# Two token tiles' k and v by seven block products in a fused attention and dense kernel

## The chip, the cores and the metric

The kernel runs on one core of a Trainium2 chip. The metric is the device time of one execution in microseconds (us), taken as the median of several runs. The core's engines work side by side, each on its own queue of instructions: PE (matrix multiply, with a separate record PEld for loading the stationary operand), DVE (vector), ACT (scalar functions), POOL (the general-purpose engine) and SP, whose queue issues nearly all DMA transfers here. PE writes into PSUM, which has eight banks of 128 partitions by 2 KB; all other on-chip data lie in SBUF.

## The reference

The input x has 2048 tokens of width 512. It is normalised per token (mean and variance over the 512 columns) and goes into two branches whose results are multiplied and added to x:

- Branch A, linear attention with 32 heads of width 16: `q, k, v = xn @ wqkv`; q and k are multiplied per head by a 16x16 matrix `w_phi`; `phi = [softmax(p), softmax(-p)]` per head, 32 values; `kv = sum over tokens of phi_k^T v` and `z = sum over tokens of phi_k`; then `num = phi_q kv`, `den = phi_q z + 1e-6`, `s = (num / den) @ wo`.
- Branch B, a dense layer: `h = xn @ w1 + b1` (1792 columns), `mish(h) @ w2`, and `silu` of that is g.
- The result is `x + s * g`.

Inputs and result are float32.

## The kernel before

**Numbers in two halves.** A float32 operand of a big matmul is kept as two tiles, high and low (`split`, line 429: ACT copies the value into the rounded type, and a subtraction gives the rest). Three matmuls (low by high, high by low, high by high) then make one exact enough product. They have the form 128x128 by 128x512. A product over the whole contraction of 512 is 4 blocks times 3, so 12 matmuls.

**The parts.** There are 16 token tiles of 128 tokens. The program is a list of parts named in the string `ORDER` (line 36), each of which records instructions:

- `wk`, `wv`, `wq`, `wo`: weights loaded, folded with `w_phi` where needed (PE), and split.
- `N t`: loads x of tile t, normalises it, transposes it on PE into the PSUM tile `pt`, splits it into the tile `xT`, copies it once more whole (`xr`), and writes the whole copy and the two halves to HBM (`raw`, `scr`).
- `K t`, `V t`, `Q t`: a projection of 12 matmuls each (`proj`, line 529). K and Q are followed by `softmax` (line 538): a copy `p` of the logits out of PSUM, a maximum and a minimum per head, two subtractions (on DVE from PSUM, or on POOL from the copy), the exponential on ACT, sums and reciprocals; for K also the scaling. `Q t` first reads its tile of xn back from HBM (`xq`).
- `A p`: for two consecutive tiles, adds phi_k to the sum `zacc` and multiplies v with phi_k into the PSUM bank `kvp` by small matmuls. `z` finishes both sums.
- `D t`: denominators, scaled phi_q, transposed on DVE in blocks of 32 into the tile `ph`, which holds four token tiles and exists once.
- `Ua g`, `Ub g`: the numerators of four token tiles in two halves of 64 small matmuls (32x32 by 32x128), then their split out of PSUM.
- `O t`: multiplication with `wo`; the result goes to HBM.
- `P b`, `M b`: w1 of two column blocks loaded, its four block sums made and split (`P`), and the halves read back from HBM later (`M`).
- `L q`: for 1024 tokens, loads xn from HBM: three blocks in halves, four blocks whole; from the whole ones four block sums are made and split.
- `Fa`, `Fb`, `Fc`, `Fd` n: the first dense layer by Strassen's scheme in Winograd's form: seven block products in place of eight, each 6 matmuls; sums of products are formed by accumulating in PSUM and by an addition on DVE (`plus`). `Fa` to `Fd` of one n hold 2, 2, 1 and 2 of the seven products.
- `R`, `G`, `E`: w2, the second dense layer with mish, and the final combination and output.

**What sets the order.** A planner in the file (`Program`) walks the parts in the order of the list. PE executes its matmuls exactly in that order. For every other instruction the planner simulates the engines with a cost per operation (line 62), gives each a due time from the PE instruction that needs it, and chooses, where an operation may run on either of two engines (`either`, `copy`), the engine. It also counts the buffers: 38 of 4 KB (`slot`), 11 of 2 KB (`s2`), 8 PSUM banks, and some smaller ones. The simulation's order is what is issued; at run time every queue is worked off in that order. All instructions are issued from one line (345), so the profile groups them by tile names.

Of the kernel before, what the change touches and what calls it, by code (L numbers as in the profile page):

```python
# [17 lines left out]
P = 128  # L18
# [14 lines left out]
SLOTS, S2 = 38, 11  # L33
# [3 lines left out]
wk0 wv1 wv0 wq0 N2 N1 P3 N0 wk1 K0 N9 N3 K2 V1 K1 V3 V2 K3 N5 N4 V0 K4 wq1 K5 A0 N8 V5 K8 K9 V4 N7 A1 P2 A2 V9 K7 N6  # L37
V8 V6 P0 N11 K6 A4 L0 V7 N10 N12 Fa3 K10 Fa0 V12 A3 V10 V11 K11 Fb3 Fb0 Fc3 Fc0 N13 N14 Fd3 K12 P6 V13 N15 P5 Fd0 K14
A5 V15 V14 K15 K13 Fa6 Fb6 Fa5 M2 Fc6 Fa2 P4 Fd6 Q5 P1 Fa4 Q2 Fb2 b1 Q1 Fc2 A6 A7 Fd2 Fa1 Fb4 Fc4 Q0 z Fb5 D1 Fb1 Fc1
D0 Q13 Q3 M4 L1 Fc5 Fd1 Q7 Q4 D4 Fd5 Q9 M0 M6 Fd4 Fa9 Fb9 Fa11 Fb11 Fc9 D3 Fc11 Fd9 Fd11 Fa7 D9 Fb7 D2 M5 D5 Fa13 Fb13  # L40
Fc13 Fc7 Fd13 Fa12 M1 Fd7 Ua0 wo0 Q6 D7 Fa8 D6 Ub0 R0 Fb8 Fb12 Fc8 Fc12 Fd8 Q8 Q12 D13 R1 Q15 wo1 M3 Fa10 Fd12 Fb10
Ua1 Fc10 Q10 Ub1 Fd10 Q14 R5 D8 D10 O0 G7 D14 O7 O4 R4 O6 G8 R2 O1 G12 Q11 O5 G9 O2 R3 G0 G3 G10 G11 R6 G13 O3 D12 D11
G1 Ua2 E1 G5 G4 G2 G6 E0 D15 G14 Ub2 G16 G15 Ua3 G18 Ub3 G19 O10 G17 O12 G20 O15 O13 O11 G21 O8 O9 O14 E2 G24 G25 G23
G22 G26 E3
# [4 lines left out]
class Op:  # L49
    __slots__ = ("impl", "reads", "writes", "at", "idx", "succ", "ndep", "late", "new", "ready", "start", "eng", "sets", "slack", "open", "soon", "pos", "deps", "lock", "part", "half", "code")  # L50


class Program:
# [53 lines left out]
    def call(self, e, m, a, k):  # L107
        aps = [v for v in list(a) + list(k.values()) if isinstance(v, bass.AP)]
        w = {aps[0].tensor.name}
        r = {v.tensor.name for v in aps[1:]}  # L110
# [36 lines left out]
    def links(self):  # L147
        ops = self.ops
        wr, rd = {}, {}
        for o in ops:  # L150
            o.succ, dep = [], set()
            for n in o.reads:
                dep.update(wr.get(n, ()))
            for n in o.writes:
                dep.update(wr.get(n, ()))
                dep.update(rd.get(n, ()))
# [6 lines left out]
            for n in o.reads:  # L163
                rd.setdefault(n, []).append(o.idx)
            for n in o.writes:
                wr.setdefault(n, []).append(o.idx)
        self.uses, self.first = {}, {}
        for o in ops:
            o.new = []
            for n in o.reads | o.writes:  # L170
                if n in self.tag:
                    self.uses[n] = self.uses.get(n, 0) + 1
                    if n not in self.first:
                        self.first[n] = o
                        o.new.append(n)

    def simulate(self, at):
# [103 lines left out]
        while left:  # L281
# [8 lines left out]
            for kind, i in todo:  # L290
# [6 lines left out]
                elif kind == 1:  # L297
                    o = ops[i]
                    left -= 1
                    for n in o.reads | o.writes:  # L300
                        if n in uses:
                            uses[n] -= 1
                            if uses[n] == 0:
                                free[self.tag[n]] += 1
# [11 lines left out]
            for e in ("A", "V", "G", "Q"):  # L316
                if busy[e] > now or e == "Q" and (dma > now + BACK or lanes[-LANES:][0:1] > [now] and len(lanes) >= LANES):
                    continue
                skip = []
                while ready[e]:  # L320
# [11 lines left out]
                    if len(skip) > 60:  # L332
                        break
# [4 lines left out]
    def issue(self):  # L338
        first = True
        for o in self.order():  # L340
            for m, a, k in o.impl[o.eng][1]:
# [3 lines left out]
                getattr(e, m)(*a, **k)  # L345

# [24 lines left out]
def block_kernel(ctx: ExitStack, tc: tile.TileContext, x, wqkT, wv, phi, wo, w1, b1, w2, out):  # L371
# [9 lines left out]
    for tag, n in (("slot", SLOTS), ("s2", S2), ("sm", 13), ("rq", 5), ("st", 3 * NT), ("tq", 1)):  # L381
        pools[tag] = ctx.enter_context(tc.tile_pool(name=tag, bufs=n))
        prog.cap[tag] = n
# [55 lines left out]
    vb = [const.tile([P, D], F32, name=f"v{i}") for i in range(4)]  # L439
# [29 lines left out]

    def fold(wT, name, i):  # L470
        hi = slot([P, 2, D], f"{name}h{i}", F32R)
        lo = slot([P, 2, D], f"{name}l{i}", F32R)
        for j in range(2):
            ps = bank([P, D], f"{name}f{i}{j}")
            with one():
                for g in range(KC):
                    PE.matmul(ps[:, g * P:(g + 1) * P], wT[2 * i + j][:, g, :], phit[:, g, :], start=True, stop=True)
            split(ps, hi[:, j, :], lo[:, j, :])
# [15 lines left out]
    scr = [dram.tile([P, 2, KC, 4, P], F32, name=f"scr{g}") for g in range(NG)]  # L494
# [411 lines left out]
```

## Time and profile before

| | |
|---|---|
| median of three runs | 521.39 us (521.24 to 522.45) |
| span of the profiled execution, first to last instruction | 520.4 us |
| its own time with what lies around the span | not recorded; the median of the runs is 1.0 us above the span |
| busy share of the span: PE, DVE, ACT, POOL | 98%, 72%, 52%, 50% |
| DMA | 120.33 MB, 231 GB/s on average |
| granted PE clock | 0.998 |

How to read it. Busy time is the time in which an engine has an instruction under way; matmuls overlap, so their mean duration (some 390 ns for 128x512) is longer than their distance. Rows of groups read: line, engine, operation, output<-inputs, shapes, count | busy us, mean ns of one | idle time of the engine just before them and what ended it. In rows of stretches each engine has its busy time in us and the number of instructions (x), then the granted clock of PE, the busy share of the DMA engines, and GB/s. The chain is the work that ended last, followed backwards; its rows are start us, length us, what.

### The profile page before, as it was taken

The numbers are of one execution on the slowest core, as the hardware profiler recorded it, in microseconds if no ns is written. First come the engines' busy times: TensorE is split into PE (matmuls) and PEld (weight loads), VectorE is DVE, ScalarE is ACT, GpSimd is POOL, SyncE is SP. The second block draws the span as 40 slices with busy tenths as digits, with TensorE's granted clock in tenths as the row PEclk, the third lists the DMA queues.
The fourth block names the chain that finished last, engine by engine and source line by source line (L and its number), as shares of the span: only waits on it lengthen the run. The fifth ranks groups of instructions, "written<-read, shape, count | busy, mean of one in ns | idle before, by whom it ended". The sixth has DMA issues, their size and how long they took to land.

```text
span 520.4 us, 9655 instructions
## 1 busy us (share of the span) xinstructions
PE 510.9 (98%) x3764; PEld 420.9 (81%) x3764; DVE 376.7 (72%) x531; ACT 270.8 (52%) x386; POOL 260.4 (50%) x160
## 2 busy tenths in 40 slices
PE   8998999999999999999999999999999999999996
PEld 8787878888888878878888878888888887888885
DVE  5999998898898977989877989957457373214304
ACT  4854566464443433552234586776496773296001
POOL 2669899677778555947543868622433310000000
PEclk9999999999999999999999999999999999999999
DMA  8888799929889789789987855674466233245802
GB/s 311 297 284 236 273 305 305 340 72 339 283 270 339 267 268 357 233 309 312 309 277 254 277 180 194 231 262 162 152 226 231 102 102 105 81 164 180 282 2 81
DMA packets 84557, 120.33 MB, mean 231 GB/s; under 512 B 7073, under 2 KB 49441, under 8 KB 84513
## 3 DMA queue, kind: packets, MB, share of 16 engines
q1 hardware_dynamic: 84368, 119.70, 68.1%
q8 instruction: 29, 0.48, 0.4%
q14 instruction: 16, 0.12, 0.1%
q10 hardware_dynamic: 144, 0.03, 0.0%
HBM read 71.08 MB, written 48.63 MB: 230 GB/s over the span
## 4 chain that ended last, share of the span: by engine, by line
PE 80%; DVE 11%; ACT 3%; POOL 2%; DMA 2%; issue 2%; ACTq 0%; POOLq 0%; DVEq 0%
PE y L345 30%; PE fx L345 13%; PE pw L345 8%; PE fy L345 6%; PE q L345 6%; PE v L345 4%; PE k L345 4%; PE fz L345 3%; PE pn L345 3%; DMA fr<-raw 2%; DVE nb L345 1%; PE wake L345 1%; PE kvp L345 1%; POOL zacc L345 1%; DVE xT L345 1%
## 5 line engine op out<-in xcount | busy, mean ns | idle before, releaser
L345 ACT ACTIVATE r<-r,b1t 128x512 f32<-128x512 f32 x56 | 38.3, 718 | 8.4 <-DMA r<-hd 8.3
L345 PE MATMUL k<-wkh,xT 128*128 128x512 f32 x128 | 42.4, 395 | 0.2 <-DVE rs L345 0.2
L345 PE MATMUL q<-wqh,xq 128*128 128x512 f32 x128 | 41.5, 390 | 0.0
L345 DVE TENSOR_TENSOR u<-u,sr 128x512 f32<-128x512 f32 (+1 forms) x14 | 10.0, 714 | 42.0 <-ACT u L345 39.5
L345 ACT ACT_TABLE_LOAD x23 | 29.5, 1283 | 1.6 <-PEq L898 1.2
L345 ACT ACTIVATE u<-y 128x512 f32<-128x512 f32 (+1 forms) x17 | 9.7, 573 | 38.5 <-PE y L345 38.4
L345 PEld LDWEIGHTS k<-wkh,xT 128*128 128x128 f32 x128 | 24.0, 188 | 6.1 <-DVE xT L345 0.8
L345 PEld LDWEIGHTS q<-wqh,xq 128*128 128x128 f32 x128 | 24.0, 188 | 5.2 <-issue 0.2
L345 PE MATMUL k<-wkl,xT 128*128 128x512 f32 x64 | 25.1, 392 | 0.0
L345 PE MATMUL q<-wql,xq 128*128 128x512 f32 x64 | 24.9, 389 | 0.0
L345 PE MATMUL v<-wv0h,xT 128*128 128x512 f32 x64 | 23.2, 403 | 0.4 <-DVE xT L345 0.4
L345 PE MATMUL v<-wv1h,xT 128*128 128x512 f32 x64 | 22.4, 390 | 0.0
L345 ACT ACTIVATE so<-pw 128x512 f32<-128x512 f32 x12 | 7.1, 596 | 26.0 <-PE pw L345 24.2
L345 DVE TENSOR_REDUCE tz<-ez 128x64 f32<-128x1024 f32 x16 | 19.2, 1198 | 0.2
L345 DVE TENSOR_TENSOR ol<-pn,oh 128x256 fp32r<-128x256 f32 x32 | 12.0, 413 | 10.1 <-ACT oh L345 10.0
L345 ACT ACTIVATE oh<-pn 128x256 fp32r<-128x256 f32 x32 | 10.6, 390 | 14.6 <-PE pn L345 9.2
L345 POOL TENSOR_TENSOR rs<-rs,mhalf 128x1 f32<-128x1 f32 x16 | 9.8, 618 | 16.1 <-DVE rs L345 16.1
L345 ACT ACTIVATE v<-v 128x512 f32<-128x512 f32 x16 | 9.4, 590 | 15.3 <-PE v L345 15.3
L345 DVE COPY so<-pw 128x512 f32<-128x512 f32 x4 | 2.8, 692 | 18.5 <-PE pw L345 18.5
L345 POOL TENSOR_TENSOR w1sl<-w1s,w1sh 128x1024 fp32r<-128x1024 f32 x5 | 12.0, 2404 | 8.3 <-ACT w1sh L345 6.8
L345 ACT ACTIVATE ha<-fx 128x512 f32<-128x512 f32 x14 | 8.4, 599 | 14.9 <-PE fx L345 12.1
L345 ACT ACTIVATE hc<-fx 128x512 f32<-128x512 f32 x14 | 8.3, 595 | 14.7 <-PE fx L345 11.8
(805 smaller groups left out, 1785.4 us busy)
## 6 DMA issues: line engine op xcount, KB each, us to landing
r<-hd SPq DMA_DIRECT2D x28, 512.0 KB, 3.8
scr<-xT SPq DMA_DIRECT2D x16, 512.0 KB, 4.8
xq<-scr SPq DMA_DIRECT2D x16, 512.0 KB, 5.4
w1b<-w1d SPq DMA_DIRECT2D x14, 512.0 KB, 5.5
w1b<-w1d SPq DMA_DIRECT2D x14, 384.0 KB, 4.7
x<-x SPq DMA_DIRECT2D x16, 256.0 KB, 4.9
raw<-xr SPq DMA_DIRECT2D x16, 256.0 KB, 4.4
fr<-raw SPq DMA_DIRECT2D x8, 512.0 KB, 7.5
```

The lines of the kernel that those rows point to most:

```text
L345: getattr(e, m)(*a, **k)
```

## The change

**k and v of two tiles by seven products.** Tiles t and t+4 form a pair. With the two halves of the contraction and with k and v as the two column halves, the eight block products become the seven of the scheme that the dense layer uses already (`kv_product`, parts `Ka`, `Kb`, `Kc`, `Kd` of pair p with 2, 2, 1 and 2 products). k of each tile and v of one get one addition (`plus`) of a PSUM bank to the copy in SBUF. The weights' four block sums are made and split in new parts `ws0` to `ws3`; they lie in the buffer `tq`, which later holds `ph`.

**x sums at norm time.** The four block sums of xn for a pair of tiles are made in `sums_x` from the PSUM tiles of both, split, kept for `Kb` to `Kd`, and written to HBM (`scrT`). `L` then only loads: three blocks and four sums, each in halves, 14 transfers of 512 KB. The whole copies `raw` are gone; the layout of `scr` is turned so that a tile's halves are contiguous.

**q logits through HBM.** `Q t` multiplies with the tile's own `xT` (no reading back of xn), copies the logits and writes them to HBM. A new part `S t` reads them and does the softmax. The softmax takes its input always from the SBUF copy, so both subtractions read SBUF, whether on DVE or on POOL.

**Numerators for eight tiles.** `ph` holds eight token tiles (32 KB). `U n` makes the numerators of half of the heads for eight tiles: 64 small matmuls 32x32 by 32x256, so there are four such parts in place of eight.

**Order and planner.** The list of parts is new. The planner now tracks which part of a tile is read and written (`box`, `meet`), and looks further past waiting operations. v tiles come from a pool of four buffers; a DMA scratch area is reduced to make room.

```
-SLOTS, S2 = 38, 11
+SLOTS, S2, RQ = 38, 11, 5
...
+wv0 wk0 wv1 ws0 N0 N1 wk1 ws1 N4 wq0 N5 Ka0 Kb0 N2 ws2 wq1 Ka1 Kc0 Q2 Ka2 N8 N6 ws3 Kd0 N3 Q5 N7 Q8 Kb1 Kc1 Q4 Ka3 N12
+Kb2 Kc2 Q0 Ka4 N9 P2 Kd2 A0 b1 Kd1 Q3 N13 N10 Q1 N11 Q6 P0 Kb3 Q13 N14 Kb4 A1 Kc3 Q10 Kc4 N15 Kd3 P1 Q7 Ka6 A2 P3 Q9
+Ka7 S4 Ka5 A3 Q14 Q11 Kd4 Kb5 Q15 Kc5 Kb6 Q12 Kd5 Kb7 Kc6 Kc7 S6 L0 A4 Fa3 P6 Kd7 Fb3 Kd6 A5 Fc3 S7 Fd3 Fa0 Fa1 Fb1 P4
+Fc1 A6 Fd1 S0 Fa4 A7 z P5 S1 D0 Fa5 M2 Fa2 Fb4 Fa6 D1 Fb0 Fc0 S2 S3 Fb6 Fd0 Fb2 Fc4 Fc6 Fd4 S5 Fb5 D2 D3 M1 L1 Fc5 Fd6
+M6 Fa9 D4 Fa8 Fc2 Fb9 Fd5 D5 Fb8 wo0 wo1 D6 M0 Fd2 Fc8 Fc9 Fd8 D7 Fd9 Fa13 U1 Fb13 Fc13 M4 U0 Fd13 S8 Fa7 O6 O1 Fb7 R2
+R0 O0 Fc7 O5 O3 O4 O7 O2 Fa11 S10 Fb11 M3 Fc11 S14 Fd7 Fa10 G7 Fd11 R3 D8 M5 R1 Fb10 Fc10 S9 D9 Fa12 R5 Fb12 Fc12 Fd10
+Fd12 R4 G0 G1 G2 G3 S11 D10 D11 S12 G8 G4 D12 S15 G9 G10 G5 R6 G6 E0 G11 S13 G12 G14 D13 G15 D14 G16 D15 G13 G17 U2 E1
+G18 U3 G19 O12 O8 O10 O14 G20 G21 G22 O15 O9 G23 O11 O13 G24 G25 E2 G26 E3
...
-    scr = [dram.tile([P, 2, KC, 4, P], F32, name=f"scr{g}") for g in range(NG)]
-    raw = [dram.tile([P, KC, 4, P], F32, name=f"raw{g}") for g in range(NG)]
+    scr = [dram.tile([P, 4, 2, KC, P], F32, name=f"scr{g}") for g in range(NG)]
+    scrT = [dram.tile([P, 4, 2, 4, 2, P], F32, name=f"scrT{q}") for q in range(2)]
+    qd = [dram.tile([P, D], F32, name=f"qd{t}") for t in range(NT)]
...
         split(pt, w[:, 0], w[:, 1])
-        xT[t] = w
+        xT[t], pts[t] = w, pt
+        g, i = divmod(t, 4)
+        Q.dma_start(scr[g][:, i], f32(w))
+        if g % 2:
+            sums_x(t - 4)
+
+    def sums_x(t):
+        p1, p2 = pts.pop(t), pts.pop(t + 4)
         xr = s2(f"xr{t}")
-        copy(xr, pt.rearrange("p k n -> p (k n)"))
-        Q.dma_start(raw[t // 4][:, :, t % 4, :], xr.rearrange("p (k n) -> p k n", k=KC))
-        Q.dma_start(scr[t // 4][:, :, :, t % 4, :], f32(w))
+        copy(xr, p2.rearrange("p k n -> p (k n)"))
+        xr = xr.rearrange("p (k n) -> p k n", k=KC)
+        ts = slot([P, 4, 2, P], f"ts{t}")
+        V.tensor_tensor(ts[:, 0], xr[:, 0:2], p1[:, 0:2], op=ALU.subtract)
+        with one():
+            V.tensor_tensor(ts[:, 1], p2[:, 2:4], ts[:, 0], op=ALU.subtract)
+            G.tensor_tensor(ts[:, 1], xr[:, 2:4], ts[:, 0], op=ALU.subtract)
+        with one():
+            V.tensor_tensor(ts[:, 2], p2[:, 2:4], xr[:, 0:2], op=ALU.subtract)
+            G.tensor_tensor(ts[:, 2], xr[:, 2:4], xr[:, 0:2], op=ALU.subtract)
+        V.tensor_tensor(ts[:, 3], p1[:, 2:4], ts[:, 1], op=ALU.subtract)
+        th, tl = (slot([P, 4, 2, P], f"t{n}{t}", F32R) for n in "hl")
+        split(ts, th, tl, either)
+        tT[t] = th, tl
+        g, i = divmod(t, 4)
+        for j, u in enumerate(tT[t]):
+            Q.dma_start(scrT[g // 2][:, i, j], f32(u))
...
+    def kv_product(ps, t, a, n, first):
+        (ah, al), (xh, xl) = w["kv"][a], combo(t, n)
+        with one():
+            for k in range(2):
+                for i, (u, v) in enumerate(((xl, ah), (xh, al), (xh, ah))):
+                    PE.matmul(ps, u[:, k], v[:, k], start=first and k == 0 and i == 0, stop=k == 1 and i == 2, skip_group_check=True)
...
-        with one():
-            V.tensor_tensor(e[:, :, 0, :], ps3, hi, op=ALU.subtract)
-            G.tensor_tensor(e[:, :, 0, :], p3, hi, op=ALU.subtract)
...
+        either(e[:, :, 0, :], p3, hi, op=ALU.subtract)
+        either(e[:, :, 1, :], lo, p3, op=ALU.subtract)
...
+    def kv_a(p):
+        t = tile_of(p)
+        x, z = bank([P, D], f"kx{p}"), bank([P, D], f"kz{p}")
+        kv_product(x, t, 0, 0, True)
+        kp[t] = held(x, f"kp{t}")
+        kv_product(z, t, 1, 1, True)
+        plus(kp[t], z)
+        k_soft(t)
+        kx[p] = [x]
...
     def q_proj(t):
-        xT[t] = slot([P, 2, KC, P], f"xq{t}", F32R)
-        Q.dma_start(f32(xT[t]), scr[t // 4][:, :, :, t % 4, :])
+        p = s2(f"qs{t}")
+        copy(p, proj(t, w["q"], "q"))
+        Q.dma_start(qd[t], p)
+
+    def q_soft(t):
+        p = s2(f"qp{t}")
+        Q.dma_start(p, qd[t])
...
+    def num(n):
+        q, i = divmod(n, 2)
+        ph = phT[q]
+        pn = [bank([P, 2, 2 * P], f"pn{n}_{b}") for b in range(4)]
...
+        fx[q] = [combo(f"b{n}", lambda u: scr[2 * q + g][:, :, u, 2 * k:2 * k + 2]) for n, g, k in ((0, 0, 0), (1, 0, 1), (2, 1, 1))]
+        fx[q] += [combo(f"t{n}", lambda u: scrT[q][:, :, u, n]) for n in range(4)]
...
-                    PE.matmul(ps, u[:, a % 3 if a < 3 else a - 3, c], v[:, k, :], start=first and k == 0 and i == 0,
+                    PE.matmul(ps, u[:, a % 3 if a < 3 else a - 3, c], v[:, :, k, :], start=first and k == 0 and i == 0,
...
+    def weights_s(i):
+        x, y, op = ((vr[0], vr[1], ALU.add), (sr[0], kr[0], ALU.subtract), (kr[0], vr[0], ALU.subtract), (kr[1], sr[1], ALU.subtract))[i]
+        sr[i] = slot([P, 2, D], f"ws{i}")
+        either(sr[i], x, y, op=op)
+        if "ws" not in w:
+            w["ws"] = alloc("tq", [P, 8, 2, D], "wss", F32R)
+        w["kv"][3 + i] = w["ws"][:, 2 * i], w["ws"][:, 2 * i + 1]
+        split(sr[i], *w["kv"][3 + i], either)
```

215 lines of the change are left out of this document (112 added, 103 removed).

## The prediction

> **What bounds the kernel now.** I read the page's head, then stretches of time, then the chain.
>
> ```profile
> span 520.4 us, 9655 instructions
> PE 510.9 (98%) x3764; PEld 420.9 (81%) x3764; DVE 376.7 (72%) x531; ACT 270.8 (52%) x386; POOL 260.4 (50%) x160
> DMA packets 84557, 120.33 MB, mean 231 GB/s; under 512 B 7073, under 2 KB 49441, under 8 KB 84513
> ```
>
> PE has work under way 98% of the span, so the time is the sum of PE's work plus the few places where it waits. Stretches show which engine could make it wait:
>
> ```profile
> core 0: us, PE busy (x) PEld busy (x) DVE busy (x) ACT busy (x) POOL busy (x), PEclk, DMA share, GB/s
> 20.00:80.00 60.00, 57.97 (x493) 46.82 (x494) 58.34 (x98) 35.29 (x56) 50.45 (x37) 1.00 0.85 277
> 80.00:258.00 178.00, 177.30 (x1067) 145.00 (x1071) 156.05 (x208) 79.07 (x116) 124.23 (x65) 1.00 0.85 285
> 0.00:258.00 258.00, 252.80 (x1653) 207.90 (x1669) 228.00 (x338) 126.41 (x187) 181.33 (x119) 1.00 0.85 285
> 258.00:521.00 263.00, 258.14 (x2128) 213.00 (x2119) 148.69 (x194) 144.42 (x199) 79.02 (x42) 1.00 0.52 178
> ```
>
> From 20 to 80 us DVE is busy 58.34 of 60 us (97%) and PE loses 2.03 us, 3.4% of it. From 80 us to the first numerators at 258 DVE is at 88% and PE loses 0.70 us of 178. After that DVE and POOL have large gaps. So PE is the bound, and DVE is what can break into it, in the front. The chain gives the price of each piece of PE work:
>
> ```profile
> 91.09 1.36 PE fz L345 x6
> 95.17 1.03 PE kvp L345 x64
> 101.86 2.72 PE k L345 x12
> 191.34 9.21 DMA fr<-raw
> 257.93 1.83 PE pn L345 x102
> 267.28 1.59 PE fx L345 x6
> ```
>
> A projection of 12 matmuls takes 2.72 us, a block product of 6 takes 1.36 us, each matmul 0.227 us. Half of a group's numerators takes 1.83 us, and the product behind it 1.59 in place of 1.36. The 9.21 us of a load in the chain did not stop PE, whose losses are those above.
>
> **The change part by part.**
>
> *k and v by seven products.* Before, 32 projections; per pair of tiles eight block products. After, seven: 8 pairs lose 1.36 us each, 48 matmuls by 0.227 = **-10.9 us** on PE. The form, 128x128 by 128x512 in halves, is unchanged, so the price is that of the rows.
>
> *Numerators.* Before 8 parts by 1.83 = 14.6 us. After 4 parts of as many matmuls, each with 256 columns moving. The price of these is in no row. Bounds: 1.83, if issuing sets the rate, and 3.66, if the columns do.
>
> ```profile
> 257.86 1.90 PE L345 MATMUL pn<-ph,kvw 32*32 32x128 f32 x128
> 6.67 1.95 PE L345 MATMUL wkf<-phit,wkT 128*128 128x128 f32 x16
> 8.46 1.95 PE L345 MATMUL wqf<-phit,wqT 128*128 128x128 f32 x16
> ```
>
> A full-array float32 record of 128 columns costs 1.79 / 16 = 112 ns (distance of the two fold groups); the small ones run at 1.83 / 128 = 14.3 ns a record. Sixteen of them fit into the array, so the columns alone would need 112 / 16 = 7 ns; twice the columns, 14 ns. That is just the present distance, so I take 2.0 us, near the lower bound: 4 by 2.0 = 8.0, **-6.6 us**. The Trainium skill weighs against this: "TensorE: Matmul & The Clock Gate", Part 3, "Measured speedup vs the span model", gives 10.6 times, not 16, for sixteen tiles at once. By it a part would take 64 by 2 by 224 / 10.6 = 2.7 us (an estimate from that page and the fold rows), and the forecast below would be 2.8 us later; the 7.8 times that this trace shows at 128 columns (112 / 14.3) stays under that and can't decide it. Four switches between small and large matmuls fewer, 0.23 us each (1.59 - 1.36): **-0.9 us**. U needs eight denominators where Ua needed four; D7 stands three parts ahead of U1, and a late D is in the term for DVE.
>
> *DVE and POOL up to the first numerators.* The rows:
>
> ```profile
> L345 DVE TENSOR_TENSOR hc<-hc,fy 128x512 f32<-128x512 f32 x14 | 9.6, 683 | 3.6 <-ACT hc L345 3.5
> L345 DVE TENSOR_TENSOR q11e<-q11e,q11r 128x1024 f32<-128x1024 f32 x1 | 1.2, 1225 | 0.0
> L345 DVE TENSOR_TENSOR q14e<-q14e,q14r 128x1024 f32<-128x1024 f32 x1 | 3.4, 3433 | 0.0
> L345 DVE TENSOR_TENSOR q2e<-q,q2m 128x512 f32<-128x512 f32 x1 | 0.7, 680 | 0.0
> L345 POOL TENSOR_TENSOR k4e<-k4m,k4p 128x512 f32<-128x512 f32 x1 | 1.1, 1060 | 0.0
> L345 DVE TENSOR_TENSOR ol<-pn,oh 128x256 fp32r<-128x256 f32 x32 | 12.0, 413 | 10.1 <-ACT oh L345 10.0
> 5.85 0.70 DVE L345 BATCH_NORM_STATS2 st<-x 128x6 f32<-128x512 f32 x1 [1.23 <-DMA x<-x]
> L345 ACT ACTIVATE xr<-pt 128x512 f32<-128x512 f32 x15 | 8.8, 602 | 3.2 <-DVE xT L345 3.2
> L345 ACT ACT_TABLE_LOAD x23 | 29.5, 1283 | 1.6 <-PEq L898 1.2
> ```
>
> Added, DVE only: 24 additions of a PSUM bank (16 for k, 8 for v), 0.68 = 16.3 us. They wait on the product and on ACT's copy; the 14 like them waited 3.6 us together, 0.26 each, and for 24 that is 6 us in which DVE's queue behind them stands; for these I count nothing more than the general loss below. Added, DVE or POOL: eight operations of 1024 for the weight sums, 1.2 = 9.8 us. Moved: the sums of x have as many elements as those that L made, but 32 of 256 columns at 0.41 = 13.1 in place of 8 of 1024 at 1.2 = 9.8, +3.3. Gone ahead of the first numerators: two n of the dense layer with their 6 additions, -4.1 (list of parts: 10 Fa in place of 12), one v split, -1.2. Later ahead of it: both wo splits, +2.4; eight softmaxes and eight denominators in place of nine and seven, about even. Net 16.3 + 9.8 + 3.3 - 4.1 - 1.2 + 2.4 = 26 us. ACT loses eight copies of xr (-4.8) and gains 4 copies of the folded weights and some splits; at half load it hides that, and also table loads of 1.28 us between exponential and mish for the eight S that stand among the G (at most 16, 20 us, in a stretch with 119 us free).
>
> PE's own way to the first numerators: 7 more Q (+19.0), two n fewer of the dense layer (14 products, -19.0), the seven products (-10.9): 258 becomes 247 us. DVE would have 228 + 26 = 254 us of work in 247: it doesn't fit unless POOL takes at least 12 us more, as it can (77 us free), at about twice the time. So DVE will stand at the 97% of the stretch from 20 to 80 until about 247, and I price it by that row: 3.4% of 227 us = 7.7 us lost, less the 2.7 that are lost there now: **+5.0 us**. Its bounds: -2.7, if nothing is lost, and +16, below. Where the loss goes once the front is over: nothing, DVE is at 57% there, and the S and D that are later now fill those gaps.
>
> *The subtractions.* 48 up to there read SBUF only, in place of PSUM on DVE. Plain cost 0.68 against about 0.6, nothing. The skill's "SBUF — State Buffer", "Who interferes with whom", says that a DVE instruction with two SBUF inputs and a POOL one that reads SBUF shut each other out for a whole instruction; q14e above, 3433 against 1225 ns for its like, agrees. This speaks against the change and is a rival below.
>
> *DMA.* The rows (KB each, us to landing; of SP's queue, what it waited for, us, times, longest):
>
> ```profile
> SPq L345 <- ACT xr L345: 13.1, 5, 5.0
> scr<-xT SPq DMA_DIRECT2D x16, 512.0 KB, 4.8
> fr<-raw SPq DMA_DIRECT2D x8, 512.0 KB, 7.5
> xq<-scr SPq DMA_DIRECT2D x16, 512.0 KB, 5.4
> raw<-xr SPq DMA_DIRECT2D x16, 256.0 KB, 4.4
> fh<-scr SPq DMA_DIRECT2D x6, 512.0 KB, 5.7
> fl<-scr SPq DMA_DIRECT2D x6, 512.0 KB, 6.4
> ```
>
> Gone: raw out and in, xq, and L's old loads: 16 by 256 KB + 8 by 512 + 16 by 512 + 12 by 512 = 22 MB. New: scrT 16 by 512 KB, q out and in 32 by 256, L 28 by 512 = 30 MB. At 285 GB/s for a share of 0.85, 335 GB/s when full, the 8 MB cost 25 us of a queue that has 0.15 of 258 = 39 us free in the front and half later. Pieces of 512 bytes become 4 KB (scr) or 1 KB (L). I take 0; bounds -1 and +9.2 (the one late load of the chain, if PE stood for it). SP's queue issues 24 transfers more; a scrT write waits there on the last split of a pair, and the x loads, w1 loads and L behind it wait too.
>
> SP stood 13.1 us for xr writes before, at no cost to PE; the writes that replace them are later by two instructions. The way of q through HBM takes some 10 us (4.8 out, 5.4 in), and S comes at least 20 parts behind its Q: hidden. The order of moving columns in Fa to Fd (four pieces of 128 in place of 512 together) is in no row for PE; DVE reads a pattern of this kind from pn at 413 ns, so I take 0; the far bound is four transposes for one matmul, which nothing suggests.
>
> *Sum.* 520.4 - 10.9 - 6.6 - 0.9 + 5.0 = 507.0 us of span; the median stands 1.0 above the span of the profiled execution (521.39 against 520.4): **508.0 us**.
>
> **The rivals.** Without the loss in the front the time is 503.0; a first numerator that starts T us in adds T - 247.
>
> *A, DVE and POOL set the front; slower.* If POOL takes nothing more, DVE's 254 us at 97% are 262, plus some 5 us until DVE's first norm (5.85): T = 267, 523.0 us. With the 24 subtractions that may fall on DVE shut out for half a POOL subtraction each (0.53 us), T = 280, 535.7. For it: DVE's 97% and q14e. Against: POOL's 77 us free, ACT at half load, much of the work is not due at once. It decides from T = 265 on; beyond 0.3% from 267. Time 519 to 536, taken at 525.
>
> *B, the numerators get no cheaper.* 4 by 3.66 = 14.6: 508.0 + 6.6 = 514.6. For it: a doubled number of columns. Against: the 7 ns above. A part of 2.7 us gives 510.8 and lies in the forecast's range.
>
> *C, loads come late.* L1 stands three parts ahead of the first product that uses it, and needs 14 buffers; if PE stands for one late load as in the chain, 508.0 + 9.2 = 517.2. Against: before, that wait cost PE nothing.
>
> *D, the front loses nothing.* 503.0 less up to 2.7: 500.3 to 503. For it: the planner places every operation, and DVE's 97% is also what a queue shows that is kept full but not late. Against: 20 to 80 us.
>
> **How the numbers follow.** Forecast (503 to 514) 0.66; A 0.12; B 0.07; C 0.06; D 0.09. Own range of the forecast 503 to 514. The range of 500 to 518 leaves out A and a little of C: about 0.13. Within 0.3% (about what a measurement of this kernel can tell from no change) means 519.8 to 523.0. A holds 0.02 of that, 0.08 above it, 0.02 below: faster 0.90, same 0.02, slower 0.08.
>
> **What would show it.** 336 matmuls of 128x512 for k and v in place of 384, at 0.227 us distance. Four pn groups of some 2.0 us in the chain; 2.7 or 3.7 would tell the bounds. DVE at 95% or more up to the first pn, which starts near 252 us; PE busy 7 to 8 us below the length of that stretch. POOL above 181 us of it. L's loads without a wait of PE behind them. Wrong would be: a first pn behind 260, PE waiting on kp additions or x sums, or on loads of L1.

## The result, and the profile after

The changed kernel takes 527.25 us (median of 4 runs, 524.62 to 529.4), the kernel before 521.32 us in the same session: a ratio of 1.0107, 95% interval 1.0075 to 1.014. It is slower by about 1.1%, where 508.0 us (500 to 518) was forecast. The profiled execution's span is 525.6 us, 5.2 us longer than before.

The head of the page after:

```profile
span 525.6 us, 8636 instructions
PE 501.0 (95%) x3204; PEld 409.6 (78%) x3204; DVE 400.7 (76%) x548; ACT 271.8 (52%) x389; POOL 301.5 (57%) x192
DMA packets 63945, 128.66 MB, mean 245 GB/s; under 512 B 7456, under 2 KB 23200, under 8 KB 63904
```

PE is busy for 9.9 us less than before (501.0 against 510.9) and the span is longer all the same: PE now stands idle for 24.6 us where it stood for 9.5. The stretches say where. First the changed kernel, up to its first numerators at 268 us and behind them, then the kernel before up to its own at 258 us (columns as in the prediction):

```profile
core 0: us, PE busy (x) PEld busy (x) DVE busy (x) ACT busy (x) POOL busy (x), PEclk, DMA share, GB/s
0.00:80.00 80.00, 68.92 (x372) 57.13 (x376) 68.38 (x130) 49.45 (x74) 62.06 (x57) 0.94 0.69 253
80.00:160.00 80.00, 79.75 (x632) 65.23 (x621) 74.18 (x100) 41.20 (x59) 72.01 (x48) 1.00 0.83 297
160.00:240.00 80.00, 74.08 (x494) 58.49 (x492) 68.85 (x90) 31.71 (x47) 58.37 (x39) 1.00 0.82 283
240.00:268.00 28.00, 24.66 (x107) 20.13 (x108) 26.91 (x40) 4.87 (x9) 14.49 (x7) 1.00 1.06 385
0.00:268.00 268.00, 247.42 (x1587) 200.97 (x1588) 238.32 (x357) 127.22 (x188) 206.94 (x148) 0.98 0.81 289
```

```profile
0.00:80.00 80.00, 75.50 (x602) 62.89 (x605) 71.95 (x131) 47.34 (x73) 57.10 (x55) 1.00 0.86 283
80.00:160.00 80.00, 80.00 (x509) 65.73 (x498) 70.26 (x88) 41.00 (x61) 61.30 (x33) 1.00 0.81 267
160.00:240.00 80.00, 79.30 (x465) 64.62 (x464) 69.12 (x97) 33.28 (x47) 50.59 (x28) 1.00 0.87 295
240.00:258.00 18.00, 18.00 (x97) 14.65 (x111) 16.66 (x25) 4.80 (x8) 12.35 (x6) 1.00 0.94 321
```

Read the second column against the first: PE stands idle for 11.08, 0.25, 5.92 and 3.34 us in the four stretches, where it stood for 4.50, 0, 0.70 and 0. The loss sits in three separate places: the start, the stretch from 160 to 240, and the last 28 us ahead of the first numerators. DVE is at 89% up to 268 us (238.32), so it is not full on the whole; in the last of the three stretches it is (26.91 of 28).

Idle time does not count matmuls that run slowly. So the distance from one start to the next beyond the normal distance of that form was added up too, over all PE instructions up to each kernel's first numerators (normal: 0.227 us for 128x512, 0.120 and 0.112 for 256 and 128 columns, 16.1 ns for the records of `kvp`, 14.3 and 21.0 ns for those of the numerators). This count, worked out from the records of both traces, each figure rounded by itself:

```
stretch, us                    before   after   more
0 to 80                           8.3    18.3   10.0
80 to 160                         0.9     1.6    0.8
160 to 240                        1.8     8.9    7.1
240 to the first numerators       0.1     3.6    3.5
sum                              11.1    32.5   21.4
```

The first numerators start at 268.4 us. Take the 21.4 off, and it is 247.0: the 247 us that the prediction worked out for PE's own way. After the front 525.6 - 268.4 = 257.2 us follow, where it was 520.4 - 257.9 = 262.5.

What PE waited for, first from 0 to 80 us, then from 150 to 268 (columns: who waited for whom, us in total, times, longest):

```profile
PE kx L345 <- ACT wss L345: 4.3, 1, 4.3
PE kx L345 <- DVE wss L345: 1.3, 1, 1.3
```

```profile
PE fy L345 <- DVE hc L345: 3.1, 1, 3.1
PE fx L345 <- DMA w1b<-w1d: 2.0, 1, 2.0
PE fy L345 <- DMA fb2l<-scr: 1.7, 1, 1.7
```

`wss` is the split sum of the weights, which the product `Kb0` needs. `fb2l` is one of the loads of `L1`, `w1b` the dense layer's weights read back. `hc` is an addition of the dense layer on DVE that frees a PSUM bank for PE.

The first of these waits has a second price. Stretches of 6 us from 18 to 36, and PE's instructions around the wait:

```profile
18.00:24.00 6.00, 1.50 (x5) 0.55 (x3) 5.93 (x10) 5.36 (x9) 6.00 (x3) 0.73 0.86 352
24.00:30.00 6.00, 4.93 (x12) 3.76 (x13) 5.98 (x8) 2.24 (x3) 6.00 (x5) 0.50 0.86 300
30.00:36.00 6.00, 6.00 (x36) 5.41 (x35) 4.11 (x11) 2.40 (x4) 6.00 (x4) 0.92 0.57 188
```

```profile
23.02 0.77 PE L345 MATMUL kx<-wss,tl 128*128 128x512 f32 x1 [4.29 <-ACT wss L345]
25.07 1.22 PE L345 MATMUL kx<-wss,th 128*128 128x512 f32 x2 [1.29 <-DVE wss L345]
26.09 0.63 PE L345 MATMUL kx<-wss,tl 128*128 128x512 f32 x1
```

PE is without work for 4.29 us up to 23.0. Within that pause the granted clock falls to 0.50 (0.73 on average from 18 to 24 us means from about 20.8 on), and it stays there until about 31 us, 8 us after PE has work again. The matmuls from 25 us on follow each other every 0.43 us in place of 0.227.

The last place, rows picked from DVE's queue ahead of the first numerators, and one of POOL's:

```profile
253.88 2.33 DVE L345 TENSOR_REDUCE tz<-ez 128x64 f32<-128x1024 f32 x2
256.40 1.21 DVE L345 TENSOR_REDUCE tz<-ez 128x64 f32<-128x1024 f32 x1
258.51 0.22 DVE L345 TENSOR_TENSOR q6r<-q6r,den 128x64 f32<-128x64 f32 x1
259.03 1.63 DVE L345 TENSOR_TENSOR q7r<-q7r,den 128x64 f32<-128x64 f32 x1
260.58 0.68 DVE L345 TENSOR_TENSOR hc<-hc,fy 128x512 f32<-128x512 f32 x1
```

```profile
258.65 1.93 POOL L345 TENSOR_TENSOR q5e<-q5e,q5r 128x1024 f32<-128x1024 f32 x1 [9.88 <-DVE den L345]
```

Three denominators are worked off one after the other (`tz` is the sum under the fraction), and only behind them comes the addition `hc`. Its product had ended at 254. PE, whose next product needs that bank, stood from 258.2 to 261.3. Of these 3.1 us, 1.4 belong to one short operation: `q7r` takes 1.63 us where `q6r`, of the same form, takes 0.22. It starts while POOL works on `q5e` and ends as that ends (260.66 and 260.58). `q7r` takes 1.63 or 1.64 us in the trace of every run of the changed kernel; no experiment moved it.

Last, the chain, for what each piece of PE work costs now:

```profile
163.46 1.36 PE fx L345 x6
268.43 2.69 PE pn L345 x116
271.11 1.58 PE fx L345 x6
```

A block product is as dear as before, with the moved columns in four pieces too. A part of the numerators takes 2.69 us, not 2.0.

### The profile page after: what moved, and what is told of

Read it like the earlier page. It is cut to its first block, busy times and chain, and to the rows that moved or that the text cites. A ratio compares the mean times of both kernels' runs of the same rounds, so it can differ in the third digit from the quotient of the medians.

```text
span 525.6 us, 8636 instructions
## 1 busy us (share of the span) xinstructions
PE 501.0 (95%) x3204; PEld 409.6 (78%) x3204; DVE 400.7 (76%) x548; ACT 271.8 (52%) x389; POOL 301.5 (57%) x192
## 4 chain that ended last, share of the span: by engine, by line
PE 78%; DVE 9%; DMA 7%; ACT 3%; issue 2%; POOL 0%; SPq 0%; DVEq 0%; ACTq 0%
PE y L345 29%; PE fx L345 9%; PE pw L345 8%; PE q L345 7%; PE kx L345 7%; PE fy L345 4%; PE ky L345 4%; PE fz L345 2%; PE pn L345 2%; DMA ft3l<-scrT 1%; DMA w1b<-w1d 1%; DMA qp<-qd 1%; DMA fb2l<-scr 1%; PE kz L345 1%; PE wake L345 1%
## 5 line engine op out<-in xcount | busy, mean ns | idle before, releaser
L345 PE MATMUL q<-wqh,xT 128*128 128x512 f32 x128 | 42.6, 395 | 0.5 <-ACT qs L345 0.3
L345 DVE TENSOR_TENSOR u<-u,sr 128x512 f32<-128x512 f32 (+1 forms) x13 | 12.6, 974 | 32.5 <-DMA sr<-so 19.6
L345 PEld LDWEIGHTS q<-wqh,xT 128*128 128x128 f32 x128 | 24.1, 188 | 6.1 <-ACT v L345 0.5
L345 PE MATMUL q<-wql,xT 128*128 128x512 f32 x64 | 25.0, 391 | 0.0
L345 PE MATMUL kx<-wss,th 128*128 128x512 f32 x64 | 20.8, 408 | 1.3 <-DVE wss L345 1.3
L345 ACT ACTIVATE hb<-fx 128x512 f32<-128x512 f32 x13 | 7.8, 600 | 22.4 <-PE fx L345 22.4
L345 PE MATMUL kx<-wss,tl 128*128 128x512 f32 x32 | 13.5, 422 | 5.7 <-ACT wss L345 4.3
L345 POOL TENSOR_TENSOR tl<-ts,th 128x1024 fp32r<-128x1024 f32 x6 | 16.3, 2718 | 2.7 <-issue 2.7
L345 ACT ACTIVATE qs<-q 128x512 f32<-128x512 f32 x16 | 9.5, 596 | 14.5 <-PE q L345 11.4
L345 PEld LDWEIGHTS kx<-wss,th 128*128 128x128 f32 x64 | 12.4, 196 | 4.2 <-DVE wss L345 1.8
L345 PE MATMUL fy<-fb2h,w1b 128*128 128x512 f32 x32 | 11.3, 394 | 3.1 <-DVE hc L345 3.1
```

## The experiments

The theory after the first look: three losses in the front, one after the other, and each a mechanism of its own. (1) The start: PE waits for the split weight sums and then runs at half clock. (2) Loads that come late between 160 and 240 us. (3) DVE's denominators, late just ahead of the first numerators. The main rival is the prediction's own step: one engine, DVE, has too much work over the whole front, and any of its work taken away gives the time back. In all experiments on the changed kernel the other instructions keep the place that the planner gave them: the edit acts only as they are issued, since the planner would otherwise place everything anew, and the edit couldn't be told from that.

Against the kernel before, the changed kernel was 1.0107 and, in the second session, 1.0113; its medians of 527.25 and 526.55 us, 526.9 on average, are what the differences below refer to.

**The additions for k and v, taken away.**

```
+                if (o.part or ' ')[0] == 'K' and m == 'tensor_tensor' and k.get('op') == ALU.add:
+                    continue
```

> The changed kernel with the plan kept, but without the 24 additions on DVE of a PSUM bank to k and v (the sums of products are left out, so k and v of half of the tiles are wrong). It takes 24 by 0.6 = 14 us of work from DVE before the first numerators. Theory 1, late transfers and a cold start (the additions only happen to lie beside): 525 to 528 us, not more than 2 us below the changed kernel (527.3), PE still standing for fb2l, w1b and hc. Theory 2, DVE and POOL set the front, as rival A of the prediction: 513 to 520 us, the first pn earlier than 260 in place of 268.

Measured: 523.63 us, 1.0052 (1.0033 to 1.0071). Rows of 0 to 80 and of 160 to 240 us:

```profile
0.00:80.00 80.00, 71.58 (x414) 59.14 (x415) 65.98 (x127) 51.17 (x77) 67.53 (x61) 0.96 0.74 274
160.00:240.00 80.00, 74.77 (x497) 58.99 (x496) 68.50 (x90) 31.82 (x47) 59.46 (x38) 1.00 0.86 300
```

16.2 us of DVE's work are gone (24 by 0.67; its busy time falls by 13.7, as others of its operations take longer) and 3.3 us of time come back: neither 2 at most, as the theory had it, nor the 7 or more of the rival. They come mostly from the start (71.58 against 68.92). The stretch from 160 to 240 still loses 5.2 us (5.9 before), and the wait for `hc` stays at 3.1. This is against the rival in its strong form: of 16.2 us of DVE's work taken away 3.3 come back, and the waits further on stay. In the start DVE's work does count.

**The low halves of L's loads, taken away.**

```
+                prog.drop = u == 1
                 Q.dma_start(f32(t), src(u))
+                prog.drop = False
...
```

(`u` is the half of a tile of `L`; the products then read the high half twice.)

> The changed kernel with the plan kept, but L reads only the high halves (7 transfers of 512 KB in place of 14, twice), and the products use the high half twice (the low part of xn is left out of the dense layer). Theory 1, late transfers: the waits of PE for ft3, fb2l, w1b and for hc behind hd writes (0.8 + 1.8 + 2.2 + 3.3 us and some of the 1.1 for ha and hb) go: 518 to 521 us. Theory 2, DVE and POOL: no gain, 525 to 529 us.

Measured: 522.68 us, 1.0024 (1.0009 to 1.0039).

```profile
160.00:240.00 80.00, 78.69 (x518) 63.29 (x517) 71.15 (x97) 33.08 (x48) 66.25 (x42) 1.00 0.79 269
240.00:262.00 22.00, 18.95 (x77) 15.20 (x76) 20.58 (x32) 2.77 (x5) 8.06 (x4) 0.92 0.84 306
```

The loss between 160 and 240 is down to 1.3 us: it was mostly the loads. PE gets to 240 earlier, and there it waits for DVE all the same, 3.05 us of 22. So the time is above the 518 to 521 expected, which had this wait go as well.

**Shorter sums on DVE.** Every reduction of 1024 elements reads half of them.

```
+                if m == 'tensor_reduce' and a[1].free_size() == 2 * D:
+                    a = (a[0], a[1][:, :, 0:DH // 2])
```

> The changed kernel with the plan kept, but every DVE sum over 1024 elements (softmax sums and denominators) reads only half of them (the other half of each sum is left out): 0.5 us less on DVE for each of some 40 up to the first numerators, 17 to 20 us of DVE. Theory 2a (transfers late up to 240 us, then DVE's denominators of eight tiles late): the last wait of 3.25 us before the first pn goes, the earlier ones for fb2l and w1b stay; first pn at 262 to 264, time 521 to 524. If DVE doesn't matter: 525 to 528.

Measured: 522.37 us, 1.0017 (1.0005 to 1.0029). PE's waits for transfers stay in part (`w1b` 2.1 us, `fb2l` 0.8 in place of 1.7); that for `hc` falls from 3.1 to 1.1:

```profile
160.00:240.00 80.00, 76.34 (x498) 60.44 (x497) 65.44 (x94) 31.48 (x46) 59.27 (x39) 0.98 0.86 297
240.00:262.00 22.00, 20.91 (x93) 16.99 (x92) 21.48 (x35) 3.98 (x7) 11.36 (x6) 1.00 1.06 388
```

**Both, the half loads and the short sums.**

> The edits of half_loads and short_sums together. Theory 2a: each edit alone uncovers the other bound; together they give more than the sum of the two alone (about 4 each): first pn at 256 to 259, time 514 to 517. If the two are independent: 518 to 520. If neither matters and the differences so far are between runs: 523 or more.

Measured: 516.37 us, 0.9899 (0.9855 to 0.9942).

```profile
160.00:240.00 80.00, 79.14 (x520) 63.69 (x519) 66.88 (x98) 33.07 (x48) 67.55 (x42) 1.00 0.79 273
240.00:262.00 22.00, 22.00 (x213) 17.25 (x212) 18.11 (x32) 4.31 (x9) 6.57 (x4) 1.00 0.83 298
```

Now nothing is lost from 240 to 262, and the first numerators start at 258.9. Alone the two edits gave 4.2 and 4.5 us, together 10.5. The surplus of 1.8 is within the interval; what shows two bounds one behind the other are the stretches: each edit alone clears most of its own stretch and leaves a loss in the other.

**Small matmuls that bridge the start.**

```
+            if o is kb[0]:
+                for _ in range(16):
+                    self.eng["PE"].matmul(ky[:, 0:P], ones, ones, start=True, stop=True)
```

> The changed kernel with the plan kept and 16 more matmuls of ones (128x128, some 3.6 us) on PE where it waits for the first weight sums, ahead of Kb0. Theory 3, the wait of 4.4 us also drops the granted clock, and the products behind it run at half rate: the granted clock from 24 to 30 us is 1.0 in place of 0.50 and the time is 3 to 4.5 us less, 523 to 524 us. Rival: the wait alone counts, and what stands behind it (DVE, POOL) would hold PE anyway: 526 to 528 us.

Measured: 522.49 us, 1.0029 (1.0013 to 1.0045). The wait for `wss` is still there, but PE has something to do in it, and no slow matmuls follow; the granted clock from 18 to 36 us is 1.00.

```profile
0.00:80.00 80.00, 74.43 (x451) 62.73 (x452) 69.75 (x139) 52.08 (x78) 69.03 (x62) 1.00 0.76 277
```

```profile
19.66 3.84 PE L347 MATMUL ky<-ones 128*128 128x128 f32 x32 [0.80 <-DVE xT L352]
```

(3.84 of the 74.43 are the sixteen matmuls themselves, each of which makes two records of 0.112 us.) 4.4 us come back from an edit that adds work. By the count above the start loses 4.5 us more than the kernel before, these matmuls included, in place of 10.0. So the half clock, and what it made late behind it, is the larger part of the start's loss. The Trainium skill, "TensorE: Matmul & The Clock Gate", Part 1, "The HAM clock gate", states that the clock falls to half after an idle window of about 3.4 us and rises again after about as long a busy one; the 0.50 behind the pause of 4.29 us agrees, though the fall came 2 us into the pause (see the last section).

**No sums of the weights.** The additions that make the sums are left out, and the splits read the folded weights.

```
+        prog.drop = True
         either(sr[i], x, y, op=op)
+        prog.drop = False
```

> The changed kernel with the plan kept, but without the four weight sums (the split takes the plain folded weights in their place, so the k and v products are wrong); the splits stay. Theory 3, the chain wv, wk, ws0, ws1, split, Kb0 sets the start: PE's wait of 4.4 us at 18.6 goes down to below 2 and the cold clock with it, 518 to 522 us. Rival, DVE and POOL are full there whatever the chain is: 525 to 528 us.

Measured: 524.5 us, 1.0068 (1.0045 to 1.0091). PE still waits before `Kb0`:

```profile
PE kx L351 <- ACT wss L351: 3.2, 1, 3.2
```

A wait of 3.2 us in place of 4.3, a clock that still falls to 0.50, and a time between the two forecasts: the sums are not all that is late. With them gone, the splits (`wss`) still come too late for a product that stands where `Kb0` stands in the list. The trace says what holds them now: ACT works without a pause from 11 to 22 us, and ahead of the split that PE waits for (20.42 us) stand five other operations, two `wqh`, `xr`, `xT` and `kp`, of 2.4 us together. In the changed kernel itself that split started as soon as its sum was there (21.70 and 21.79), so there the sum and ACT's queue end together.

**All three: half loads, short sums, small matmuls.**

> short_half with the 16 matmuls of ones that keep the clock up at the start: 3 to 4 us less again, 510 to 514, first pn at 252 to 255, if the start is a loss of its own; the same as short_half, if the start only shifts when the other bounds hit.

Measured: 514.86 us, 0.9878 (0.9851 to 0.9906); the first numerators start at 255.1 us. With the three losses treated the changed kernel is 12.0 us faster than it was. The forecast of 508.0 is 6.9 below that: 2.8 of it are the numerators, and most of the rest is the start, where PE is still idle for 6.9 us of 80 (4.5 in the kernel before) and has the added matmuls to do.

```profile
0.00:80.00 80.00, 73.11 (x443) 61.64 (x444) 70.55 (x138) 51.51 (x77) 66.56 (x61) 1.00 0.73 270
```

**The changed kernel once more, beside these.**

> The changed kernel once more, beside the three others on the same chip: 525 to 528 us, first pn at 266 to 269 us.

Measured: 526.55 us, 1.0113 (1.0086 to 1.014), first numerators at 267.8 us: the same result in another session.

**Fewer writes of dense weights.** Are the loads late because the DMA engines are full, or because a buffer or SP's queue holds them?

```
+            prog.drop = b != 2
             Q.dma_start(d[:, 0:n], f32(t)[:, 0:n])
+            prog.drop = False
...
```

(`M` then reads block 2 for all blocks.)

> The changed kernel, every operation where it was, but the copies of the split first dense weights are written to HBM for one block alone and the later parts all read that block (results are wrong in the dense layer; about 5 MB of writes between 169 and 212 us are gone). If the late loads (fb2l and w1b, PE waits of 1.7 to 2.2 us each) are late because the DMA engines are full, these waits go and PE is busy 77 of 80 us in 160 to 240: 521 to 524 us, held up by the denominators after. If they are late because their buffers come free late or because SP's queue stands ahead of them, the waits stay as they were: 526 to 528 us.

Measured: 523.17 us, 1.0031 (1.0009 to 1.0053). The bytes fall by 11.0 MB to 117.64, and PE's waits from 150 to 268 us are all for DVE, with one short one for ACT:

```profile
160.00:240.00 80.00, 76.94 (x508) 61.10 (x507) 72.26 (x94) 32.19 (x47) 62.34 (x41) 1.00 0.71 238
240.00:262.00 22.00, 18.96 (x77) 15.25 (x76) 21.49 (x33) 3.38 (x6) 10.39 (x5) 0.93 1.04 367
```

```profile
PE fy L351 <- DVE hc L351: 3.0, 1, 3.0
PE fz L351 <- DVE hb L351: 1.8, 1, 1.8
```

Both waits for transfers are gone. `fb2l` was issued only 0.6 us earlier (168.2 in place of 168.8) but landed after 5.2 us in place of 6.8, and no PE wait follows it; the share of the DMA engines from 170 to 180 us is 0.83 in place of 1.01 (the changed kernel's row, then that of this one):

```profile
170.00:180.00 10.00, 7.66 (x32) 5.69 (x33) 9.61 (x9) 6.17 (x9) 6.42 (x5) 1.00 1.01 375
```

```profile
170.00:180.00 10.00, 9.31 (x40) 7.07 (x39) 9.59 (x9) 6.55 (x10) 7.63 (x7) 1.00 0.83 285
```

So for this load the full DMA engines are the best account. For `w1b` it isn't settled: it is issued 3.5 us earlier (208.5 in place of 212.0), since SP has fewer transfers ahead of it and the work before it ran earlier, and in this kernel it also doesn't have to wait for its own block to be written. And again the time that is won up to 240 is partly lost to DVE behind it.

**Numerators with the loops exchanged.**

```
-                    for m in range(4):
-                        h = 16 * i + 8 * c + 2 * m + s
-                        for b in range(4):
+                    for b in range(4):
+                        for m in range(4):
+                            h = 16 * i + 8 * c + 2 * m + s
```

> The changed kernel with the two inner loops of the numerators exchanged: the sixteen 32x32 products of a round are issued down one strip of banks after another in place of across them (same work, nothing left out). If sixteen products at once are bounded by the array (columns that move), a part stays at 2.69 us: 525 to 528 us. If it is the order in which neighbours share rows or columns of the array, it changes by up to 0.7 us a part either way: 2.0 us, about 524, or 3.4 us, about 529.

Measured: 526.88 us, 1.0115 (1.0092 to 1.0138), as the changed kernel. A row of its chain, beside 2.69 there:

```profile
267.11 2.69 PE pn L345 x118
```

The order in which the sixteen places of the array are visited makes no difference to a part. 2.69 / 128 is 21.0 ns from one record of 32x256 to the next, against 14.3 ns for 32x128 (the prediction's row of 128 in 1.83 us): twice the columns for 1.47 times the time.

**Eight tiles for the numerators alone, on the kernel before.** Only `U` and `ph` for eight tiles; U0 and U1 stand where Ua1 and Ub1 stood, U2 and U3 where Ua3 and Ub3 stood.

```
-            phT[g] = alloc("tq", [P, H, 4, 32], f"ph{g}")
+            phT[g] = alloc("tq", [P, H, 8, 32], f"ph{g}")
...
```

> The kernel before with one part of the change alone: numerators for eight tiles (four U of 128 records with 256 columns in place of eight half parts with 128), all else as before; its list of parts names U0 and U1 where Ua1 and Ub1 stood and U2, U3 where Ua3 and Ub3 stood, and every operation is placed anew. Nothing is left out. If the gain belongs to the part itself, four parts by the 2.69 us of the changed kernel take the place of eight by 1.83 (-3.9) and four transitions of 0.23 go (-0.9): 516.6 us, ratio about 0.991. If eight denominators ahead of the first U, or the new placing, eat it: 520 to 524. If the part costs 3.66 without the changed kernel's surroundings: 520.5.

Measured: 518.27 us (5 runs, 517.81 to 519.06), 0.9944 (0.9931 to 0.9956). This beats both kernels, by less than the 516.6 expected. A part in the chain, and what PE waited for in the numerators:

```profile
290.12 2.68 PE pn L338 x116
```

```profile
PE pn L338 <- DVE ol L338: 1.5, 1, 1.5
```

PE's busy time is 505.7 us, 5.2 less than before: the -3.9 and -0.9 of the expectation are there. 1.5 us of them go to a new wait: a part now takes four banks for itself, and U1 stands until DVE's splits (`ol`) have freed those of U0.

**A bridge at the start, and one addition ahead of the denominators.** Nothing is left out here; the rest of D5, D6 and D7 is issued behind the addition of `Fc8` and not ahead of it.

```
+        late = [o for o in od[od.index(first5):i] if o.part in ("D5", "D6", "D7")]
+        od = [o for o in od[:i] if o not in late] + [fc] + late + od[i + 1:]
```

> The changed kernel with the sixteen small matmuls ahead of the first product on the weight sums (as in warm_start), and one exchange on DVE's queue: the addition hc that PE's bank waits for, which stood behind the last steps of the denominators D5, D6, D7 (sums with r, reciprocals, products: some 4.4 us of DVE's time), is issued ahead of them. Nothing is left out and no work is taken away. If the order of DVE's queue makes PE's wait for hc, that wait (3.1 us) falls below 1 us, the denominators end 0.7 us later, and the first numerators start about 2 us earlier than in warm_start: 262 us in, 520 to 521 us in all. If it is DVE's total work that is late, the wait moves to the denominators of the numerators themselves, and the time stays at warm_start's 522 to 523 us.

Measured: 521.03 us (10 runs), 1.0008 (0.9986 to 1.0029), against 1.0029 for the bridge alone; the spans are 519.2 and 521.1.

```profile
PE fy L357 <- DVE hc L357: 2.2, 1, 2.2
```

```profile
253.22 1.25 DVE L357 STREAM_TRANSPOSE ph<-q5e 128x1024 f32<-128x1024 f32 x1
254.39 0.65 DVE L357 TENSOR_TENSOR hc<-hc,fy 128x512 f32<-128x512 f32 x1
```

The profiled span is shorter by the 2 us expected, but by another way. The wait of 3.1 us for the addition of `Fc8` is gone; then PE waits 2.2 us for the next such addition (`Fc9`), which stands behind a transpose. PE reaches the numerators at 259.4 in place of 264.0, where their first part stretches to 5.3 us with a pause of 1.4 (the trace doesn't say for what), and it ends at 264.7 in place of 266.7. So the order on DVE's queue decides which result PE waits for, and each wait removed is followed by another. What the exchange is worth in time is not shown: the medians differ by 1.5 us, with intervals that overlap, and of the shorter span some 2 us lie ahead of 240 us, where the exchange changes nothing. With nothing left out, the changed kernel with both edits comes to the time of the kernel before, not below it.

## Why the prediction was wrong, point by point

**What bounds the kernel: right.** PE stayed the bound. By the terms below its work fell by 15.7 us; its busy time fell by 9.9 only, as slow matmuls and the ends of waits count as busy. What the forecast had wrong is how well PE can be kept supplied.

**k and v by seven products, -10.9 us: right.** A product takes 1.36 us as in the rows before. Without the losses of the count above PE's way to the first numerators is 257.9 - 11.1 = 246.8 us before and 268.4 - 32.5 = 235.9 after: 10.9 less.

**Numerators, -6.6 us: mis-sized.** A part takes 2.69 us, so four take 10.8 in place of 14.6: -3.9. I had taken 2.0, near the lower bound, by the argument that sixteen products at once need 7 ns a column step of 128 and that 14 ns fit into the present distance. They don't run sixteen abreast: 64 by 2 by 224 ns / 2.69 us is 10.7. The Trainium skill, "TensorE: Matmul & The Clock Gate", Part 3, "Measured speedup vs the span model", gives 10.6, which the prediction weighed and did not take, as it called the trace's 7.8 undecided; this trace agrees with it. The 2.8 us are the smaller error. The four transitions, -0.9, are right (1.58 behind `pn`, 1.36 elsewhere), and the part by itself is worth having, as the kernel with it alone shows.

**The loss in the front, +5.0 us: the step that failed.** It took one row (PE loses 3.4% while DVE is 97% busy) as the rate of loss for the whole front, as if all of it were alike. Measured are 21.4 us, nearly all of it in three places with three causes:

- 0 to 80 us, 10.0 us: `Kb0` needs the split sums of weights that `wk` and `wv` have only just made. I had priced their operations (8 by 1.2 us on DVE or POOL) and not the latency of the first product that waits for them. The price was low as well: ahead of `Kb0` those on DVE took 1.75 to 2.45 us and those on POOL 2.4 to 3.35. PE's pause of 4.3 us then halves its clock until 8 us behind the pause. `warm_start` gives 4.4 us of this back.
- 160 to 240 us, 7.1 us: loads of `L1` and of the dense weights come late. `half_loads` and `few_writes` take these waits away; by the same count `half_loads` gets 5.6 us of it back.
- 240 to 268 us, 3.5 us: eight denominators are needed where four were, D5 to D7 come at the end, and the additions that free PE's banks stand behind them. `short_sums` shows it; in `warm_add_first` this wait goes and a shorter one takes its place. `q7r`, held up beside POOL, is 1.4 us of it.

The 0.8 us from 80 to 160 I did not follow. The sum by these terms: 520.4 - 10.9 - 3.9 - 0.9 + 21.4 = 526.1; the span is 525.6. The losses in the front belong to one list of parts and one placing by the planner; no run tried another list with the whole change, so it isn't shown that the change itself must lose them. My bounds for this term were -2.7 and +16; the measured one is outside.

**DVE and POOL, 26 us more work: right in sum, wrong in what it does.** Up to the first numerators DVE has 238.3 us (+10.3) and POOL 206.9 (+25.6): the work went to POOL at about the price that I had named. DVE at 95% or more up to there was my sign for the step, and it is at 89%. No engine's total decided, but the time at which a few results were due.

**DMA, 0 us: wrong.** The +8.3 MB are right. My argument was that the queue has 39 us free. But that is an average: the share of busy DMA engines is 1.01 from 170 to 180 us, where `fb2l` is on its way, and 1.06 from 240 to 268. The term's upper bound (+9.2) holds what the loads cost (5.6 us by `half_loads`).

**D7 three parts ahead of U1, "a late D is in the term for DVE": wrong.** It is an effect of its own, by the place of a few operations on one queue.

**The rivals.** A (slower, DVE and POOL set the front) gave T = 267 and 523.0 us, against 268.4 and 527.25. So its time was near, but by luck: its reason, that POOL takes nothing and DVE is full, isn't what happened. B is half true: 2.69 lies between 1.83 and 3.66. C, the late loads, is true, at some 5.6 us in place of 9.2. D is out. The chances treated A, B and C as if only one of them could come; they came together, with a fourth, the start, that I had not seen.

**The subtractions that read SBUF only, 0 us: open.** No experiment took them apart. The traces show a cost: up to the first numerators no addition or subtraction of 128x512 on DVE took more than 0.70 us in the kernel before, and in the changed kernel six of these subtractions took 0.95 to 2.0, some 4 us too much together. What that cost in time is not shown.

## What to carry to other kernels

When an edit takes work from the bound engine, count for the stretch ahead of each new consumer: which result does it need first, how long is the chain to that result, and what stands ahead of it on each queue on the way. Averages (DVE at so many per cent, DMA with so many us free) say whether the work fits, not whether it comes in time; use them per stretch of some 10 us around each new dependency. And try the parts of a compound change singly: here one small part on the old kernel gave 3.0 us (ratio 0.9944), while the whole lost 5.9.

## What was unexpected of the hardware

**A pause costs twice, and where it falls decides.** A pause of 4.29 us on PE left the granted clock at 0.50 until 8 us behind it. But the length alone does not decide. With a pause of 3.09 us each ahead of the same product, the changed kernel kept its clock, and the one with small matmuls at the start did not. The 4 us behind the pause, in the changed kernel and in `warm_start`:

```profile
262.00:266.00 4.00, 4.00 (x20) 3.26 (x18) 3.73 (x5) 0.00 (x0) 2.38 (x2) 1.00 1.06 365
```

```profile
256.00:260.00 4.00, 4.00 (x14) 3.11 (x13) 3.73 (x5) 0.00 (x0) 2.38 (x2) 0.64 1.06 384
```

What else decides can be worked out from the clock records of the traces (start and length of each stretch at one granted clock). In each of the fourteen traces, all changes of the clock lie whole multiples of 3.41 us apart: at 20.77 and 31.01 us in the changed kernel, at 255.45 and 258.86 in `warm_start`. Cut each trace into pieces of 3.41 us on that grid, and add up in each piece the time in which PE has nothing under way. From full speed, the clock was at 0.50 behind all 19 pieces with 1.88 us or more, and stayed at 1.00 behind all others, of which the emptiest had 1.86. The pause of `warm_start` (252.23 to 255.32) lies in one piece; that of the changed kernel (258.22 to 261.31) is parted at 259.70 into 1.48 and 1.61. And in `short_sums` a pause of 2.09 us, all in one piece, was enough; behind it:

```profile
217.00:220.00 3.00, 3.00 (x8) 2.32 (x7) 1.60 (x3) 0.60 (x1) 1.36 (x2) 0.50 1.06 363
```

So the same pause costs the clock in one run and not in another, by where the grid lies. The ends of matmuls are modelled in the trace, so the bound of some 1.87 us is good for this count alone. The Trainium skill, "TensorE: Matmul & The Clock Gate", Part 1, "The HAM clock gate", has the activity measured in windows of about 3.4 us that run on by themselves, and the clock fall after an idle one; the traces agree on the windows, but a window did not have to be idle as a whole.

**Full DMA engines do not mean one rate.** Where the changed kernel's `fb2l` comes late (170 to 180 us) their share is 1.01 at 375 GB/s, and in the last stretch ahead of the numerators 1.06 at 385, while the mean over the span is 245. The prediction had taken 335 GB/s for full. But in `warm_start` they are as full from 30 to 36 us, with a share of 0.99, at 269 GB/s. So the share tells whether a load has room, not the rate.

**DVE and POOL can hold each other up.** `q7r` on DVE took 1.63 us in place of 0.22 and ended with the operation on POOL that it had started beside (see the last place in the front). `q14e` in the kernel before, which the prediction shows, is alike: it started at 331.89 us, 0.03 behind one on POOL of 2.39 us, and took 3.43 us in place of 1.2.
